# Normalising u on three engines instead of one: statistics on VectorE and GpSimd, scaling on ScalarE, modulation on VectorE, in pairs of blocks

## The chip, the cores and the metric

The kernel runs on one core of a Trainium2 chip. Its time is the device time of one execution in microseconds; each comparison takes the median of some runs of each kernel on the same chip. Traces come from one profiled execution.

## What is computed

A token mixer (a state-space convolution, "S4") and a channel mixer, each behind a layer norm that is modulated by a condition vector. Cut to what matters here:

```python
x = A_u                                              # 1 x 2048 x 512
mod = (silu(c) @ w_mod).reshape(1, 6, 1, -1)
sa, ca, ga, sb, cb, gb = (mod[:, k] for k in range(6))
h = layernorm(x) * (1 + ca) + sa                     # the part that the change touches
x = x + ga * ssm(h, ...)                             # K = Re sum C exp(dt A l) dB; y = irfft(rfft(K) rfft(h)) + h Dskip
h = layernorm(x) * (1 + cb) + sb
x = x + gb * mixer(h, w1, w2, w3, w4)                # shifts, two matmuls, two more with gelu
```

## The kernel before

The convolution is done in the frequency domain, with the transforms as matmuls. **The first stage** (to about 213 us of the span) makes the kernel K of the convolution and the first transform of u; the stages behind it (spectra, inverse transform, mixer, channel matmuls) begin with the last matmuls of the first and are not touched.

The order of the instructions is written out by hand (`tc.manual_schedule()`): each engine runs its own list from front to back, and an instruction that waits holds up all behind it. The first stage is a loop over 33 steps `k`. In step k stand, in this order:

- what an earlier step has put into `later` (on ScalarE, "ACT": the eviction `KX<-kp` of the last bursts, the evictions `vs<-pu` of a transform of u with their stores to VU, the modulation's rows `wm` and `modg`);
- `turns(k + 2)`: 18 matmuls on TensorE ("PE", lines 457 and 458) into two PSUM tiles `xx` (two buffers), and two sines on ACT, `tr<-xx`, that read them;
- in steps 1, 5, 9, ... 25 the exponentials for the next four steps: five times two matmuls (lines 251 and 256) and five activations `p<-xx`, a table load before and one behind them, with some matmuls of `fill` (line 491) that keep PE busy;
- `products(k)` on VectorE ("DVE"): two operations at line 475, in even steps one at 481, and one each at 484 and 485; they write `e0` and `e1` (two buffers each);
- `burst(k)` on PE: 64 small matmuls (line 507) that read them;
- after step 3, 7, ... 27 a small product of weights on DVE (line 263, `weigh`);
- `side[k]`: work hung on this step by a table.

u is held as 16 blocks of 128 x 512, four to a tile `ut[g]` ("xu"), two tiles at a time. Per block `side` has `u_stats` (DVE: `bn_stats`, `bn_aggr`, lines 146 and 147; GpSimd, "POOL": add eps and a power, lines 149 and 150), two steps later `u_norm` (DVE, lines 424 and 425: subtract the mean and multiply by 1 + ca, multiply by 1/sigma and add sa), and per pair of blocks two transforms `u_dft` (PE, line 434), one in each of the next two steps. When the second pair and the fourth pair have been transformed, `load_u` reloads the tile (four transfers of 256 KB on SyncE's queue, line 237). The steps:

```python
at = lambda i: 1 + (i * 28) // 16
for i in range(16):
    side[max(at(i) - 2, 0)].append(lambda i=i: u_stats(i))
    side[at(i)].append(lambda i=i: u_norm(i))
    if i % 2 == 1:
        side[at(i) + 1].append(lambda i=i: u_dft(i - 1, 0))
        side[at(i) + 2].append(lambda i=i: u_dft(i - 1, 1))
    if i % 4 == 3 and i < 8:
        side[at(i) + 2].append(lambda i=i: load_u(i // 4 + 2))
```

Behind step 31's products PE runs eight warming matmuls (line 497), the last burst and four more.

Of the kernel before, what the change touches and what calls it, by code (L numbers as in the profile page):

```python
# [7 lines left out]
F32 = mybir.dt.float32  # L8
F32R = mybir.dt.float32r
I32 = mybir.dt.int32  # L10
AF = mybir.ActivationFunctionType
OP = mybir.AluOpType
# [94 lines left out]
def dram(t, off, ap):  # L107
    return bass.AP(tensor=t.tensor, offset=t.offset + off, ap=ap)


def body(ctx, tc, A):
    nc = tc.nc
    V, S, P, T, Y = nc.vector, nc.scalar, nc.gpsimd, nc.tensor, nc.sync
    pool = lambda name, bufs=1, **k: tc.tile_pool(name=name, bufs=bufs, **k)
    glob = ctx.enter_context(pool("glob"))
    dpool = ctx.enter_context(pool("dscr", space=DRAM))

    def act(out, in_, f=AF.Copy, scale=1.0, bias=0.0):
        return S.activation(out, in_, f, bias=bias, scale=scale)  # L119
# [11 lines left out]
    eps_t = glob.tile([128, 8], F32, name="eps_t")  # L131
    V.memset(eps_t, 1e-5)
    pw = glob.tile([128, 8], F32, name="pw")
    V.memset(pw, -0.5)
    m_one = glob.tile([128, 8], F32, name="m_one")
    V.memset(m_one, -1.0)
    mv1 = glob.tile([128, 16, 2], F32, name="mv1")
    rs1 = glob.tile([128, 16], F32, name="rs1")
    st1 = glob.tile([128, 10, 2, 6], F32, name="st1")

    def ln_stats(pl, xs, tag):
        n = len(xs)
        st = pl.tile([128, n, 6], F32, name=tag + "s")
        mv = pl.tile([128, n, 2], F32, name=tag + "m")
        for i, x in enumerate(xs):
            V.bn_stats(st[:, i], x)
            V.bn_aggr(mv[:, i], st[:, i])
        r = pl.tile([128, n], F32, name=tag + "r")
        P.tensor_tensor(r, mv[:, :, 1], eps_t[:, :n], op=OP.add)
        P.tensor_tensor(r, r, pw[:, :n], op=OP.pow)  # L150
        return mv, r

    def exp_exact(pl, x, shape, name, scale=1.0):
        t = lambda s, dt=F32: pl.tile(shape, dt, name=f"{name}_{s}")
# [47 lines left out]
    mods = [modu[:, k] for k in range(3)] + [modg[:, k] for k in range(3)]  # L202
# [29 lines left out]
    ut = {}  # L232

    def load_u(g):
        x = ut[g] = up.tile([128, 4, 512], F32, name="xu")
        for bp in range(4):
            Y.dma_start(x[bp * 32:(bp + 1) * 32],
                        dram(A["u"], (bp * 16 + g * 4) * 512, [[64 * 512, 32], [1, 2048]]))
# [45 lines left out]
    with tc.manual_schedule():  # L284
# [89 lines left out]
        at, at0 = tmp("at"), tmp("at0")  # L374
# [36 lines left out]
    wk = a1.enter_context(pool("wk", bufs=2, reuse_waits="tile"))  # L411
# [4 lines left out]
    ul = {}  # L416

    def u_stats(b):
        ul[b] = ln_stats(wk, [ut[b // 4][:, b % 4]], "lu")

    def u_norm(b):
        x = ut[b // 4][:, b % 4]
        mv, r = ul.pop(b)
        V.scalar_tensor_tensor(x, x, mv[:, 0, 0:1], mods[1], op0=OP.subtract, op1=OP.mult)
        V.scalar_tensor_tensor(x, x, r[:, 0:1], mods[0], op0=OP.mult, op1=OP.add)

    def u_dft(b, cp2):
        x = ut[b // 4]
        ps = [psu.tile([128, 512], F32, name="pu") for h in range(2)]
        for i in range(2):  # L430
            for h in range(2):
                q = 64 * (1 - i if h == 0 else i)
                j = slice(32 * JB[2 * h + cp2], 32 * JB[2 * h + cp2] + 32)
                T.matmul(ps[h][q:q + 64], FU[j, h, cp2 * 64:cp2 * 64 + 64], x[j, b % 4 + i],
                         start=True, stop=True, skip_group_check=True)

        def evict():
            vs = uv.tile([128, 2, 512], F32, name="vs")
            for h in range(2):
                act(vs[:, h], ps[h])  # L440
                c0 = h * 32 + cp2 * 16 + (14 - b if h == 0 else b)
                for i in range(2):
                    Y.dma_start(dram(VU, (c0 + i) * 256, [[16384, 64], [1048576, 2], [1, 256]]),
                                vs[i * 64:i * 64 + 64, h].rearrange("p (a d) -> p a d", a=2))
        later.append(evict)
# [69 lines left out]
    side = {k: [] for k in range(40)}  # L515
    for k in range(8):
        w, i = ("w3", k) if k < 4 else ("w4", k - 4)
        n = A[w].shape[0] // 4
        side[4 + 3 * k].append(lambda w=w, i=i * n, n=n: P.dma_start(WD[w][i:i + n], A[w][i:i + n]))
    for n in range(3, 6):  # L520
        k = 7 * n - 9
# [1 line left out]
        side[k].append(lambda n=n: later.append(mod_parts(n)))  # L523
        side[k + 1].append(lambda n=n: later.append(mod_sum(n)))
    at = lambda i: 1 + (i * 28) // 16
    for i in range(16):
        side[max(at(i) - 2, 0)].append(lambda i=i: u_stats(i))
        side[at(i)].append(lambda i=i: u_norm(i))
        if i % 2 == 1:
            side[at(i) + 1].append(lambda i=i: u_dft(i - 1, 0))  # L530
            side[at(i) + 2].append(lambda i=i: u_dft(i - 1, 1))
        if i % 4 == 3 and i < 8:
            side[at(i) + 2].append(lambda i=i: load_u(i // 4 + 2))

    def add_skip(h, g0, g1):
        V.tensor_add(Kq[:, h, g0:g1, 31], DS[:, h * 64 + g0:h * 64 + g1], Kq[:, h, g0:g1, 31])
# [114 lines left out]
    def spectrum_k(jh, kc):  # L651
        p = [psa.tile([128, 2, 2, 128], F32, name="pk2") for gh in range(2)]
        for i in range(2):
            for ro in range(2):
                for ri in range(2):
                    for kk in range(2):
                        for gh in range(2):
                            k1 = kc * 4 + 2 * kk + i
                            rows = slice(gh * 64, gh * 64 + 64)
                            w = T2[k1 // 16][rows, k1 % 16]  # L660
                            if ri == gh:
                                w = w[:, ro * 64:ro * 64 + 64]
                            elif ro == ri:
                                w = w[:, gh * 64:gh * 64 + 64]
                            else:
                                w = T3[rows, k1]
                            T.matmul(p[gh][kk * 64:kk * 64 + 64, i, ro], w,
                                     VK[jh][rows, ri * 32 + k1].rearrange("p j g -> p (j g)"),
                                     start=(ri == 0), stop=(ri == 1), skip_group_check=True)
        return p  # L670
# [115 lines left out]
    def transposed(x):  # L786
        ps = [psT.tile([128, 2, 256], F32, name=f"pT{j}") for j in range(2)]
        for k in range(4):
            for i in range(2):
                T.transpose(ps[k // 2][:, k % 2, i * 128:i * 128 + 128], x[:, i, k * 128:k * 128 + 128], ident)  # L790
        return ps

    def parts_of(ps):
        hi = [cm.tile([128, 2, 256], F32R, name=f"nh{j}") for j in range(2)]
        lo = [cm.tile([128, 2, 256], F32R, name=f"nl{j}") for j in range(2)]
        for j in range(2):
            act(hi[j], ps[j])
            V.tensor_sub(lo[j], ps[j], hi[j].bitcast(F32))  # L798
        return [hi[k // 2][:, k % 2] for k in range(4)], [lo[k // 2][:, k % 2] for k in range(4)]
# [283 lines left out]
    with tc.manual_schedule():  # L1083
# [12 lines left out]
        for n, st in enumerate(steps):  # L1096
            p = spectrum_k(*st)
# [126 lines left out]
        n = cm.tile([128, 2, 512], F32, name="h2")  # L1224
        sm = [(cm.tile([128, 2], F32, name="cmv"), cm.tile([128, 1], F32, name="crs")) for i in range(2)]
# [17 lines left out]
        r = transposed(n)  # L1243
        split_w(1)
        r = parts_of(r)
# [4 lines left out]
        for g in range(8):  # L1250
            r = chan(g, r)
# [18 lines left out]
```

## Time and profile before

| | |
|---|---|
| median of 3 runs | 717.22 us (712.0 to 718.76) |
| the profiled execution | 716.82 us, span 715.1 us |
| PE matmul, PE weight load | 671.7 us (94%), 520.1 us (73%) |
| DVE | 506.3 us (71%) |
| ACT | 335.6 us (47%) |
| POOL | 85.6 us (12%) |
| granted PE clock | 0.993 on average |

The shares are means over the span. In the first stage DVE, ACT and PE are all far busier than the means of DVE and ACT say, so a table of stretches of 20 us is read before the page's totals. In timelines each row has its start in us, its length in us, engine, line, operation, output and input, the count, and in brackets the idle time before it with what ended it. Line 119 is the helper of all activations; these are told apart by their tiles.

### The profile page before, as it was taken

The numbers are of one execution on the slowest core, as the hardware profiler recorded it, in microseconds if no ns is written. First come the engines' busy times: TensorE is split into PE (matmuls) and PEld (weight loads), VectorE is DVE, ScalarE is ACT, GpSimd is POOL, SyncE is SP. The second block draws the span as 40 slices with busy tenths as digits, with TensorE's granted clock in tenths as the row PEclk, the third lists the DMA queues.
The fourth block names the chain that finished last, engine by engine and source line by source line (L and its number), as shares of the span: only waits on it lengthen the run. The fifth ranks groups of instructions, "written<-read, shape, count | busy, mean of one in ns | idle before, by whom it ended". The sixth has DMA issues, their size and how long they took to land.

```text
span 715.1 us, 16869 instructions
## 1 busy us (share of the span) xinstructions
PE 671.7 (94%) x7083; PEld 520.1 (73%) x7083; DVE 506.3 (71%) x847; ACT 335.6 (47%) x549; POOL 85.6 (12%) x191
## 2 busy tenths in 40 slices
PE   2689999999999899998899999999999999999997
PEld 1356655666568566664688889989898998989896
DVE  8989999999986566767978868557463635454422
ACT  2768898889956255634245623313123121212121
POOL 1011212112000001100463200201010000000000
PEclk9999999999999999999999999999999999999999
DMA  8452274744439999793649402011020111111011
GB/s 286 152 129 69 74 217 102 191 128 116 132 80 266 232 289 315 224 324 144 217 149 302 132 5 56 15 45 31 16 74 16 49 27 31 31 30 30 0 30 31
DMA packets 56884, 85.52 MB, mean 120 GB/s; under 512 B 5764, under 2 KB 43656, under 8 KB 55144
## 3 DMA queue, kind: packets, MB, share of 16 engines
q1 hardware_dynamic: 52648, 66.61, 34.8%
q0 software_dynamic: 3136, 16.52, 6.4%
q10 hardware_dynamic: 1024, 1.31, 0.6%
q8 instruction: 56, 0.92, 0.5%
q14 instruction: 20, 0.16, 0.1%
HBM read 58.20 MB, written 31.85 MB: 126 GB/s over the span
## 4 chain that ended last, share of the span: by engine, by line
PE 48%; DVE 2%; ACT 1%; DMA 1%; SPq 0%; issue 0%; POOL 0%; DVEq 0%; ACTq 0%
PE pm L825 7%; PE pm L828 7%; PE pm L826 7%; PE pa L949 6%; PE pa L941 6%; PE pa L942 5%; PE ph L879 2%; PE ph L880 2%; PE ph L882 2%; PE pT L790 2%; DMA ld<-ZT 1%; PE pT L1140 1%; PE py L722 1%; ACT nh L119 0%; DVE st L758 0%; SPq L707 0%
## 5 line engine op out<-in xcount | busy, mean ns | idle before, releaser
L119 ACT ACTIVATE gh<-pm 128x512 fp32r<-128x512 f32 (+1 forms) x48 | 26.9, 560 | 200.7 <-PE pm L828 200.7
L825 PE MATMUL pm<-nh,w3h 128*128 128x256 f32 (+1 forms) x352 | 85.8, 279 | 0.9 <-ACT nh L119 0.9
L826 PE MATMUL pm<-nh,w3l 128*128 128x256 f32 (+1 forms) x352 | 85.6, 279 | 0.1
L933 DVE TENSOR_TENSOR gl<-gf,gh 128x512 fp32r<-128x512 f32 (+1 forms) x48 | 30.8, 642 | 68.4 <-ACT gf L119 68.4
L941 PE MATMUL pa<-w4h,gh 128*128 128x512 f32 (+1 forms) x176 | 69.6, 396 | 0.0
L942 PE MATMUL pa<-w4l,gh 128*128 128x512 f32 (+1 forms) x176 | 68.9, 392 | 0.0
L825 PEld LDWEIGHTS pm<-nh,w3h 128*128 128x128 f32 (+1 forms) x352 | 65.3, 185 | 2.6 <-ACT nh L119 1.1
L826 PEld LDWEIGHTS pm<-nh,w3l 128*128 128x128 f32 (+1 forms) x352 | 65.2, 185 | 2.2 <-DVE w3l L744 0.5
L828 PE MATMUL pm<-nl,w3h 128*128 128x256 f32 (+1 forms) x352 | 54.8, 277 | 0.0
L949 PE MATMUL pa<-w4h,gl 128*128 128x512 f32 (+1 forms) x176 | 48.1, 391 | 0.8 <-DVE gl L933 0.8
L458 PE MATMUL xx<-MG,ON 64*128 64x512 f32 x160 | 48.0, 396 | 0.0
L457 PE MATMUL xx<-MG,ON 64*128 64x512 f32 x160 | 48.0, 396 | 0.0
L828 PEld LDWEIGHTS pm<-nl,w3h 128*128 128x128 f32 (+1 forms) x352 | 46.7, 185 | 0.2 <-DVE nl L798 0.2
L753 POOL TENSOR_TENSOR rs<-mv,eps_t 128x1 f32<-128x1 f32 (+1 forms) x39 | 11.4, 293 | 279.0 <-DVE mv L759 266.6
L678 DVE TENSOR_TENSOR ma<-pk,us 128x512 f32<-128x512 f32 x32 | 21.9, 685 | 30.7 <-issue 22.9
L119 ACT ACTIVATE z<-pz 128x512 f32<-128x512 f32 x32 | 17.5, 595 | 54.6 <-PE pz L693 38.3
L885 DVE TENSOR_TENSOR h<-h,ph 128x512 f32<-128x512 f32 x16 | 11.0, 686 | 45.2 <-PE ph L882 45.2
L475 DVE SCALAR_TENSOR_TENSOR e<-tr,p 128x512 f32<-128x512 f32 x64 | 41.0, 682 | 2.1 <-ACT tr L119 1.9
L949 PEld LDWEIGHTS pa<-w4h,gl 128*128 128x128 f32 (+1 forms) x176 | 33.0, 188 | 8.3 <-DVE gl L933 1.2
L484 DVE TENSOR_TENSOR e<-tr,p 128x1024 f32<-128x1024 f32 x32 | 38.9, 1217 | 0.0
L507 PEld LDWEIGHTS kp<-e,e 128*32 128x32 f32 x2048 | 30.0, 110 | 12.2 <-issue 8.1
L485 DVE TENSOR_TENSOR e<-tr,m 128x1024 f32<-128x1024 f32 x32 | 38.9, 1216 | 0.0
(234 smaller groups left out, 1763.5 us busy)
## 6 DMA issues: line engine op xcount, KB each, us to landing
VU<-vs SPq DMA_DIRECT2D x64, 128.0 KB, 3.5
ld<-VU SPq DMA_DIRECT2D x32, 256.0 KB, 10.4
ZT<-z POOLq DMA_DIRECT2D x15, 512.0 KB, 8.3
ld<-ZT SPq DMA_DIRECT2D x12, 512.0 KB, 8.2
Dw<-in_w POOLq DMA_DIRECT2D x8, 688.0 KB, 4.7
xu<-in_u SPq DMA_DIRECT2D x16, 256.0 KB, 6.8
KX<-in_u SPq DMA_DIRECT2D x16, 256.0 KB, 10.2
GD<-go SPq DMA_DIRECT2D x16, 256.0 KB, 2.3
```

The lines of the kernel that those rows point to most:

```text
L119: return S.activation(out, in_, f, bias=bias, scale=scale)
L457: T.matmul(x[:, :512], la, ma, start=(i == 0), stop=(i == len(ops) - 1))
L458: T.matmul(x[:, 512:], lb, mb, start=(i == 0), stop=(i == len(ops) - 1))
L475: V.scalar_tensor_tensor(e0[:, 1, a], tr[:, 1, 0], 1.0 - 2.0 * a, mg[:, a], op0=OP.mult, op1=OP.mult)
L484: V.tensor_mul(e0[:, 0], tr[:, 0, 0:1].to_broadcast([128, 2, 512]), mg)
L485: V.tensor_mul(e1.rearrange("p r d q -> p r (d q)"), tr[:, :, 1], m1s[0][:, u % 2:u % 2 + 1].to_broadcast([128, 2, 512]))
L825: T.matmul(p, wh[:, k, c], hi[k], start=(k == 0), stop=False)
L826: T.matmul(p, wl[:, k, c], hi[k], start=False, stop=False)
L828: T.matmul(p, wh[:, k, c], lo[k], start=False, stop=(k == 3))
L941: T.matmul(acc[i], gh[:m, e, s], W4h[:m, f], start=(f == 0), stop=False)
L942: T.matmul(acc[i], gh[:m, e, s], W4l[:m, f], start=False, stop=False)
L949: T.matmul(acc[i], gl[:m, e, s], W4h[:m, f], start=False, stop=(f == 10))
```

## The change

The normalising is done per pair p of blocks (2p, 2p + 1), eight pairs. DVE only runs `bn_stats`; POOL makes mean and variance from its two halves, 1/sigma, and minus mean over sigma, in ten small operations; ACT applies both to each block (`u_scale`, Identity with a scale and a bias per partition, in place); DVE multiplies the pair by 1 + ca and adds sa in two operations of 128 x 1024 (`u_mod`). The pair's steps: statistics in step q and the one behind it (the first pair's both in step 0), scaling in step o - 1, modulation in step o, transforms in o + 1 and o + 2, reload in o + 2 for the pairs 1 and 3. q is 0, 1, 3, 7, 11, 14, 17, 21 and o is 5, 7, 9, 13, 16, 20, 23, 27. So the first pair's transforms go from steps 3 and 4 to 6 and 7, the second's from 7 and 8 to 8 and 9, and its reload from 8 to 9; all other transforms stay.

```diff
+    lnc = glob.tile([128, 5], F32, name="lnc")
+    for i, v in enumerate((0.5, 1.0 / 512, 1e-5, -0.5, -1.0)):
+        V.memset(lnc[:, i:i + 1], v)
...
     def u_stats(b):
-        ul[b] = ln_stats(wk, [ut[b // 4][:, b % 4]], "lu")
-
-    def u_norm(b):
-        x = ut[b // 4][:, b % 4]
-        mv, r = ul.pop(b)
-        V.scalar_tensor_tensor(x, x, mv[:, 0, 0:1], mods[1], op0=OP.subtract, op1=OP.mult)
-        V.scalar_tensor_tensor(x, x, r[:, 0:1], mods[0], op0=OP.mult, op1=OP.add)
+        p, i = divmod(b, 2)
+        if i == 0:
+            ul[p] = [wk.tile([128, 2, n], F32, name=f"lu{n}", bufs=3) for n in (6, 2, 1, 3)]
+        st, sm, d, rn = ul[p]
+        V.bn_stats(st[:, i], ut[b // 4][:, b % 4])
+        if i == 1:
+            t = lambda o, x, y, op: P.tensor_tensor(o, x, y, op=op)
...
+            t(rn[:, :, 0:1], rn[:, :, 0:1], c(3), OP.pow)
+            t(rn[:, :, 2:3], sm[:, :, 0:1], c(4), OP.mult)
+            t(rn[:, :, 1:2], rn[:, :, 2:3], rn[:, :, 0:1], OP.mult)
+
+    def u_scale(p):
+        rn = ul.pop(p)[3]
+        for i in range(2):
+            x = ut[p // 2][:, p % 2 * 2 + i]
+            act(x, x, AF.Identity, scale=rn[:, i, 0:1], bias=rn[:, i, 1:2])
+
+    def u_mod(p, k, op):
+        x = ut[p // 2][:, p % 2 * 2:p % 2 * 2 + 2]
+        V.tensor_tensor(x, x, mods[k][:, None].to_broadcast([128, 2, 512]), op=op)
...
-    for i in range(16):
...
+    for p in range(8):
+        o = at(2 * p + 1) + (3, 1, 0, 0, 0, 0, 0, 0)[p]
+        q = (0, 1, 3, 7, 11, 14, 17, 21)[p]
+        side[q].append(lambda p=p: u_stats(2 * p))
+        side[q + (p > 0)].append(lambda p=p: u_stats(2 * p + 1))
+        side[o - 1].append(lambda p=p: u_scale(p))
+        side[o].append(lambda p=p: u_mod(p, 1, OP.mult))
+        side[o].append(lambda p=p: u_mod(p, 0, OP.add))
+        side[o + 1].append(lambda p=p: u_dft(2 * p, 0))
+        side[o + 2].append(lambda p=p: u_dft(2 * p, 1))
+        if p in (1, 3):
+            side[o + 2].append(lambda p=p: load_u(p // 2 + 2))
```

How ACT's list stands around step 22, behind the exponentials of step 21 (`TABLE_LOAD`, `turn`): before,

```order
L119 ACT_TABLE_LOAD
L119 ACTIVATE turn_370<-hpi 128x1
L119 ACTIVATE KX<-kp 128x8x64
L119 ACTIVATE vs<-pu 128x512 x2
L119 ACTIVATE tr<-xx 128x1024
L119 ACTIVATE tr<-xx,hpi 128x1024
L119 ACTIVATE vs<-pu 128x512 x2
```

and with the change:

```order
L119 ACT_TABLE_LOAD
L119 ACTIVATE turn_376<-hpi 128x1
L119 ACTIVATE KX<-kp 128x8x64
L119 ACTIVATE vs<-pu 128x512 x2
L119 ACTIVATE tr<-xx 128x1024
L119 ACTIVATE tr<-xx,hpi 128x1024
L119 ACTIVATE xu<-xu,lu_1998 128x512 x2
L119 ACTIVATE vs<-pu 128x512 x2
```

The two `tr` are the sines of step 24. The scaling of pair 6 (`xu<-xu,lu`) has come in behind them; pairs 1 and 7 stand in the same way behind the sines of steps 8 and 28.

DVE's list between the products of steps 23 and 24, before,

```order
L485 TENSOR_TENSOR e_2428<-tr,m_2350 128x1024
L263 TENSOR_TENSOR p_2232<-p_2232,WN 128x64x4
L424 SCALAR_TENSOR_TENSOR xu<-xu,lum,modu 128x512
L425 SCALAR_TENSOR_TENSOR xu<-xu,lur,modu 128x512
L146 BN_STATS lus<-xu 128x6
L147 BN_AGGR lum<-lus 128x2
L475 SCALAR_TENSOR_TENSOR e_2499<-tr,p_2236 128x512 x2
```

and with the change (line 497 is 485 of before, 254 is 263, 487 is 475, 437 is `u_mod`):

```order
L497 TENSOR_TENSOR e_2464<-tr,m_2375 128x1024
L254 TENSOR_TENSOR p_2259<-p_2259,WN 128x64x4
L437 TENSOR_TENSOR xu<-xu,modu 128x1024 x2
L487 SCALAR_TENSOR_TENSOR e_2528<-tr,p_2263 128x512 x2
L493 TENSOR_TENSOR m_2532<-p_2259 128x1024
```

One block's normalising and another's statistics have made room for the modulation of a pair, which stands ahead of step 24's products.

SyncE's queue from the second pair's stores to the reload of the first tile, before,

```order
L443 DMA VU<-vs 64x2x256 x12
L213 DMA wm<-in_wm 128x4x512
L237 DMA xu<-in_u 32x2048 x4
L443 DMA VU<-vs 64x2x256 x16
L213 DMA wm<-in_wm 128x4x512
```

and with the change:

```order
L455 DMA VU<-vs 64x2x256 x8
L204 DMA wm<-in_wm 128x4x512
L455 DMA VU<-vs 64x2x256 x4
L228 DMA xu<-in_u 32x2048 x4
L455 DMA VU<-vs 64x2x256 x16
L204 DMA wm<-in_wm 128x4x512
```

The reload of u (`xu<-in_u`) has gone four stores further back, to behind the transform of step 9, and no longer follows the 1 MB load of `wm` directly.

More of the change, by code (lines that the diff above doesn't have):

```diff
@@ L139, in body @@
     st1 = glob.tile([128, 10, 2, 6], F32, name="st1")
[L141 to L151, printed above, removed]
     def exp_exact(pl, x, shape, name, scale=1.0):
@@ L418, in u_stats @@
     def u_stats(b):
-        ul[b] = ln_stats(wk, [ut[b // 4][:, b % 4]], "lu")
-    def u_norm(b):
-        x = ut[b // 4][:, b % 4]
-        mv, r = ul.pop(b)
-        V.scalar_tensor_tensor(x, x, mv[:, 0, 0:1], mods[1], op0=OP.subtract, op1=OP.mult)
-        V.scalar_tensor_tensor(x, x, r[:, 0:1], mods[0], op0=OP.mult, op1=OP.add)
+        p, i = divmod(b, 2)
[5 more added lines that the diff above has]
+            t = lambda o, x, y, op: P.tensor_tensor(o, x, y, op=op)
+            c = lambda q: lnc[:, None, q:q + 1].to_broadcast([128, 2, 1])
+            t(sm, st[:, :, 1:3], st[:, :, 4:6], OP.add)
+            t(sm, sm, lnc[:, None, 0:2].to_broadcast([128, 2, 2]), OP.mult)
+            t(d, st[:, :, 1:2], st[:, :, 4:5], OP.subtract)
+            t(d, d, c(0), OP.mult)
+            t(d, d, d, OP.mult)
+            t(rn[:, :, 0:1], sm[:, :, 1:2], d, OP.add)
+            t(rn[:, :, 0:1], rn[:, :, 0:1], c(2), OP.add)
+            t(rn[:, :, 0:1], rn[:, :, 0:1], c(3), OP.pow)
[9 more added lines that the diff above has]
+        V.tensor_tensor(x, x, mods[k][:, None].to_broadcast([128, 2, 512]), op=op)
     def u_dft(b, cp2):
@@ L525, in body @@
     at = lambda i: 1 + (i * 28) // 16
-    for i in range(16):
[L527 to L533, printed above, removed]
+    for p in range(8):
[10 more added lines that the diff above has]
+            side[o + 2].append(lambda p=p: load_u(p // 2 + 2))
     def add_skip(h, g0, g1):
```

## The prediction

> **What bounds the kernel now.** I read the table of stretches first. The change sits in the first stage, which ends at about 213 us with the last burst of matmuls. Columns: PE, PEld, DVE, ACT and POOL busy, PEclk, DMA.
>
> ```profile
> 80.00:100.00 20.00, 19.34 (x352) 12.95 (x353) 19.67 (x29) 16.75 (x21) 5.39 (x8) 0.91 0.46 133
> 120.00:140.00 20.00, 19.96 (x358) 12.72 (x346) 19.70 (x26) 17.96 (x23) 3.63 (x6) 1.00 0.50 140
> ```
>
> DVE is busy 19.7 of 20 us, PE 19 to 20, ACT 17 to 18: three engines are nearly full at once. Which of them sets the end is read from the timeline at the end of the stage.
>
> ```profile
> 209.78 1.21 DVE L485 TENSOR_TENSOR e<-tr,m 128x1024 f32<-128x1024 f32 x1
> 207.93 1.10 PE L507 MATMUL kp<-e,e 128*32 128x64 f32 x64
> 208.96 2.11 PE L497 MATMUL xx<-CE,TES 128*128 128x512 f32 x8
> 211.04 1.10 PE L507 MATMUL kp<-e,e 128*32 128x64 f32 x64
> ```
>
> DVE's last product ends at 209.78 + 1.21 = 210.99, and the last burst starts at 211.04. But PE comes to it from eight warming matmuls that end at 211.07: both arrive together. So DVE and PE bound the stage jointly, and a shorter DVE alone leaves PE's list where it is.
>
> Below, P(k) is step k's products on DVE, burst(k) the matmuls that read them, tr(k) the two sines of step k, which ACT makes in step k - 2. In steps 1, 5, 9, ... 25 ACT also does five exponentials between two table loads, so that tr(8), tr(24) and tr(28), made right after such a block, come latest.
>
> **The change part by part.**
>
> ```profile
> L424 DVE SCALAR_TENSOR_TENSOR xu<-xu,lum,modu 128x512 f32<-128x512 f32 x16 | 11.9, 743 | 0.0
> L425 DVE SCALAR_TENSOR_TENSOR xu<-xu,lur,modu 128x512 f32<-128x512 f32 x16 | 12.0, 752 | 1.8
> L147 DVE BATCH_NORM_AGGREGATE lum<-lus 128x2 f32<-128x6 f32 x16 | 2.9, 182 | 0.6
> L146 DVE BATCH_NORM_STATS2 lus<-xu 128x6 f32<-128x512 f32 x16 | 11.0, 685 | 0.0
> L484 DVE TENSOR_TENSOR e<-tr,p 128x1024 f32<-128x1024 f32 x32 | 38.9, 1217 | 0.0
> L119 ACT ACTIVATE h<-h,nm,rs 128x512 f32<-128x512 f32 x16 | 12.8, 813 | 26.8 <-POOL nm L815 26.8
> L150 POOL TENSOR_TENSOR lur<-lur,pw 128x1 f32<-128x1 f32 x16 | 13.9, 872 | 1.3
> L149 POOL TENSOR_TENSOR lur<-lum,eps_t 128x1 f32<-128x1 f32 x16 | 8.5, 531 | 149.3 <-DVE lum L147 149.3
> 358.54 1.51 ACT L119 ACTIVATE h<-h,nm,rs 128x512 f32<-128x512 f32 x2
> ```
>
> DVE loses 16 x (743 + 752 + 182) ns = 26.8 us and gets 16 products of 128x1024; L484 has the same shape and also a broadcast operand, 1217 ns: 19.5 us. Saved: 7.3 us. The statistics stay at 685 ns a block. ACT gets 16 activations with scale and bias from SBUF; the later stage has the very form (h<-h), two in 1.51 us, so 8 x 1.51 = 12.1 us on an engine with some 2 us free in 20. It needs no new table load: ACT's list has 18 before and after. Pool gets ten small operations a pair, nine at about 0.53 and a power at 0.87: some 5.6 us, hidden behind the three or more steps (of about 5.2 us) between statistics and scaling; without that cover the scaling would wait those 5.6 us. The early statistics therefore remove a wait for Pool. The five constants are memsets of the prologue, costed at nothing beside its loads.
>
> What is added on the path is another wait: DVE's modulation of pair p now waits for ACT's scaling, and ACT's list has the scaling of pairs 1, 6 and 7 right behind tr(8), tr(24) and tr(28), the late ones. Behind the waiting modulation stands P(8), P(24) or P(28), whose sines are by then long there. So such a P starts after tr's end + 1.51 (scaling) + 2.5 (two dependent products: 1.22 + 1.22 and the gap of 0.1 that stands below between L424's end and L425) = 4.0 us. Step 24 as it is:
>
> ```profile
> 171.46 0.42 DVE L263 TENSOR_TENSOR p<-p,WN 128x256 f32<-128x256 f32 x1
> 171.79 0.74 DVE L424 SCALAR_TENSOR_TENSOR xu<-xu,lum,modu 128x512 f32<-128x512 f32 x1
> 172.65 0.75 DVE L425 SCALAR_TENSOR_TENSOR xu<-xu,lur,modu 128x512 f32<-128x512 f32 x1
> 172.95 1.14 ACT L119 ACTIVATE tr<-xx,hpi 128x1024 f32<-128x1024 f32 x1
> 173.95 1.12 ACT L119 ACTIVATE vs<-pu 128x512 f32<-128x512 f32 x2
> 174.14 1.28 DVE L475 SCALAR_TENSOR_TENSOR e<-tr,p 128x512 f32<-128x512 f32 x2
> 177.61 1.22 DVE L485 TENSOR_TENSOR e<-tr,m 128x1024 f32<-128x1024 f32 x1
> 179.06 1.10 PE L507 MATMUL kp<-e,e 128*32 128x64 f32 x64
> ```
>
> DVE fills the time from 171.46 + 0.4 with normalising and starts P(24) at 174.14, as tr(24) ends (172.95 + 1.14 = 174.09). P(24) ends at 178.83, burst(24) follows at 179.06: 0.2 us to spare. After: 174.09 + 4.0 + 4.7 (P's length, 174.14 to 178.83) = 182.8, so burst(24) is some 3.7 us later. Steps 8 and 28:
>
> ```profile
> 70.11 1.09 PE L434 MATMUL pu<-xu,FU 32*64 32x512 f32 x8
> 82.72 1.01 ACT L119 ACTIVATE tr<-xx 128x1024 f32<-128x1024 f32 x1
> 91.66 1.10 PE L507 MATMUL kp<-e,e 128*32 128x64 f32 x64
> 194.57 1.14 ACT L119 ACTIVATE tr<-xx,hpi 128x1024 f32<-128x1024 f32 x1
> 194.73 1.29 DVE L475 SCALAR_TENSOR_TENSOR e<-tr,p 128x512 f32<-128x512 f32 x2
> ```
>
> Step 8: the two transforms of the first pair (the second at 70.11, 1.0 us each to the next start) move from steps 3 and 4 to 6 and 7, so PE, and ACT behind it, reaches step 5's exponentials 2.0 us earlier. The second tr(8) then ends at 82.72 + 0.9 + 1.0 - 2.0 = 82.6; scaling and modulation bring 86.6, one block's statistics (0.7) 87.3, P(8) 92.0, against burst(8) at 91.66: the head start is gone, **+0.4 us**.
>
> Step 12: the load of the third group of u waits for the second pair's last transform, which moves from step 8 to step 9, where it stands behind the exponentials' matmuls; and the statistics that need this load move up from step 13 to 11.
>
> ```profile
> 97.91 1.10 PE L507 MATMUL kp<-e,e 128*32 128x64 f32 x64
> 101.91 0.51 PE L251 MATMUL xx<-CE,TES 128*128 128x512 f32 x2
> 113.66 1.10 PE L507 MATMUL kp<-e,e 128*32 128x64 f32 x64
> 95.00 2.04 SPq L237 DMA_DIRECT2D xu<-in_u  x4
> DMA to landing us min/median/max: 4.9/6.8/7.7
> ```
>
> Burst(9) at 97.91 + 0.4 = 98.3, exponentials to 102.42 + 0.4 = 102.8, transform to 103.9, the last of four issues 1.5 us on at 105.4. Landing takes 4.9 to 7.7 us; I take 5.8, below the median, since the 1 MB load of weights that goes right before this one now goes four stores earlier: 111.2. DVE stands until then. Statistics 0.7, P(12) 4.7: 116.6 against burst(12) at 113.66, **+2.9 in all, 2.5 of it new**. The fourth group's load (issued in step 15, wanted in step 17) is as tight as this; I take nothing for it, and at most the third's 2.5.
>
> Step 24: 174.09 + 2.9 + 4.0 + 4.7 = 185.7 against 179.06, **+6.6, 3.7 new**. Step 28: tr(28) ends at 195.71, + 6.6 + 4.0 = 206.3 against P(28)'s start at 194.73, **+11.6, 5.0 new**. From there DVE has only products, 194.73 to 210.99 before, and the last burst waits for them: the stage ends 11.6 us late. The 7.3 us that DVE saves lie in its waits. The later stages start from that burst and shift whole.
>
> **Bounds.** The scaling pair costs 1.12 (the vs pair above) to 1.63 us (two of 0.813): -1.2 to +0.4 over three places. The landing at 4.9 or 7.7 us: -0.9 or +1.9, and the fourth load 0 to +2.5. Then PE's clock:
>
> ```profile
> 80.00:82.00 2.00, 1.82 (x10) 1.51 (x12) 1.97 (x6) 1.98 (x3) 1.00 (x2) 0.63 0.00 0
> 82.00:84.00 2.00, 2.00 (x10) 1.13 (x8) 2.00 (x3) 1.73 (x4) 0.98 (x2) 0.52 0.67 220
> 244.49 0.61 PE L667 MATMUL pk<-VK,xu 64*64 64x128 f32 x4 [3.12 <-issue]
> 244.00:246.00 2.00, 1.51 (x29) 0.59 0.96 228
> 246.00:248.00 2.00, 2.00 (x42) 0.56 1.01 336
> ```
>
> The granted clock is about 0.55 for 3.5 us after a gap of 3.12 us in stage two, and once in this stage without such a gap; half a clock for 3.5 us costs PE about 1.6 us. The change gives PE waits of 2 to 4 us at bursts 8, 12, 24 and 28, each of them a candidate. I take one such stretch beyond those of before, **+1.5**, with none to four as ends (0 to +6.2).
>
> [...]
>
> **Sum.** 0.4 + 2.5 + 3.7 + 5.0 + 1.5 = 13.1 us. The profiled execution took 716.82 us (span 715.1), the median of the runs is 717.22: 716.82 + 13.1 = **729.9**.
>
> **Rivals.**
> *No further half clock* (0.20): 11.6 alone, 728.4. For it: waits here are mostly under 3.12 us.
> *A half clock after every wait* (0.14): 11.6 + 4 x 1.5 = 17.6, 734.4. For it: those two stretches; against: at step 28 DVE sets the end and hides it.
> *The waits are absorbed* (0.20): ACT has 2 to 3 us free in 20; if scaling lands in that free time, or PE is far enough behind DVE at these bursts, only the 2.9 of step 12 is left: 719.7. Against: at bursts 24 and 31 the slack is 0.2 and 0.0.
> *The saving arrives* (0.08, the other side): DVE would end 7.3 us earlier, at 709.5 if PE followed. PE can't follow that far: its rows stand end to end but for two waits for ACT at each of seven exponential blocks,
>
> ```profile
> 97.25 0.73 PE L256 MATMUL xx<-CE,TES 32*128 32x512 f32 x2 [0.46 <-ACT tr L119]
> 102.76 0.50 PE L457 MATMUL xx<-C,T0S 64*128 64x512 f32 x1 [0.34 <-ACT p L119]
> ```
>
> so 7 x 0.8 = 5.6 us in all. Half of that gives 714.0. It decides if tr(24) and tr(28) come over 4 us earlier against DVE than now.
> *The change doesn't do what it says*: the statistics are indeed early, but the modulation waits for the scaling, which is not; this is the forecast's mechanism.
>
> **Chances.** The forecast with one stretch has 0.38. A measurement of this kernel can tell about 1%, 7.2 us, from no change (the three runs spread from 712.0 to 718.76). Slower by over 1% (above 724.4) are the forecast and the first two rivals, 0.72; faster by over 1% (below 710) only the extreme of the last, 0.03; within 1% 0.25. The likeliest case's own range is 725 to 736; with the absorbed case in it the range is 717 to 736.
>
> **What would show it.** Right: DVE, gap-free before, idle 2 to 7 us before the modulations of pairs 1, 6 and 7, released by ACT xu, and 3 to 5 us before the statistics of step 11, released by the load; PE waiting on DVE's products at bursts 8, 12, 24 and 28; the stage ending near 225 us; ACT with 16 activations xu<-xu of 0.8 us; Pool about 22 us busier, waited for by nobody. Wrong: DVE still at 19.7 of 20, or a last burst before 215 us.

## The result and the profile after

The changed kernel takes **741.71 us** (median of 4 runs, 735.49 to 743.66) against 717.22 before: ratio **1.034** (95% interval 1.030 to 1.038). Run again in a later comparison it took 738.49 us against 717.37, ratio 1.026 (1.019 to 1.033). One of those four runs, 743.03 us, counts as slow and is left out of the ratio and of the means below. The profiled execution took 735.49 us, span 733.7, granted clock 0.984 (before: 716.82, 715.1, 0.993). Slower was foretold; the median lies 11.8 us above the forecast and 5.7 above the range.

In the changed file the products stand at lines 487 to 497 (before 475 to 485), the bursts at 519 (507), the warming matmuls at 509 (497), statistics, Pool's chain and modulation at 414, 416 and 437. The table of stretches, after; columns PE, PEld, DVE, ACT, POOL busy, PEclk, DMA:

```profile
80.00:100.00 20.00, 17.25 (x284) 11.07 (x280) 17.72 (x21) 14.94 (x21) 6.34 (x3) 0.83 0.46 130
120.00:140.00 20.00, 17.63 (x287) 10.75 (x291) 19.97 (x24) 18.48 (x24) 14.11 (x14) 1.00 0.24 68
200.00:220.00 20.00, 17.37 (x293) 10.34 (x286) 13.80 (x16) 16.14 (x21) 0.00 (x0) 0.97 0.12 30
```

Before, the last slice that lies wholly in the stage was:

```profile
180.00:200.00 20.00, 19.52 (x305) 11.41 (x296) 19.60 (x26) 18.13 (x23) 1.45 (x2) 1.00 0.32 78
```

Where three engines were nearly full, PE now has 17 to 18 of 20 us. DVE has 17.7 in the first of these slices and 13.8 in the last, with the waits of steps 8 and 28; between 120 and 140 us it is as full as before. The groups of the first stage, after: busy, mean ns of one, then idle before and its releaser.

```profile
L437 DVE TENSOR_TENSOR xu<-xu,modu 128x1024 f32<-128x1024 f32 x16 | 19.6, 1223 | 11.1 <-ACT xu L119 10.8
L119 ACT ACTIVATE xu<-xu,lu 128x512 f32<-128x512 f32 x16 | 12.3, 828 | 0.0
L414 DVE BATCH_NORM_STATS2 lu<-xu 128x6 f32<-128x512 f32 x16 | 10.9, 684 | 13.1 <-DMA xu<-in_u 13.1
L416 POOL TENSOR_TENSOR lu<-lu 128x2 f32<-128x2 f32 (+1 forms) x32 | 41.5, 1297 | 92.8 <-DVE lu L414 91.5
```

The prices of the operations came as taken: 19.6 us for the products on DVE (taken 19.5), 12.3 for ACT's scaling (12.1). What is new is the idle time: DVE waits 10.8 us for ACT's scaling, at three places, and 13.1 us for two loads of u. The table of waits (total, times, longest) carries this over to PE:

```profile
PE kp L519 <- DVE e L497: 13.2, 6, 3.2
```

The end of the stage, from the timeline:

```profile
229.04 1.22 DVE L497 TENSOR_TENSOR e<-tr,m 128x1024 f32<-128x1024 f32 x1
228.53 2.10 PE L509 MATMUL xx<-CE,TES 128*128 128x512 f32 x8
230.56 1.10 PE L519 MATMUL kp<-e,e 128*32 128x64 f32 x64
```

The last burst starts at 230.56, 19.5 us later than before; 18.6 us of that is in the span. So the loss of the profiled execution lies in the first stage. The starts of single bursts (rows kp<-e,e of 64 matmuls in the timelines) show where it arises. The last three columns are counted from burst(0), which itself lies between 48.66 and 51.98 us in the profiles of this document:

| burst | before, us | after, us | after later by | new since the row above | foretold |
|---|---|---|---|---|---|
| 0 | 48.66 | 49.69 | 0 | | |
| 8 | 91.66 | 92.94 | 0.25 | 0.25 | 0.4 |
| 9 | 97.91 | 102.18 | 3.24 | 3.0 | 1.5, place open |
| 12 | 113.66 | 121.89 | 7.20 | 4.0 | 2.5 |
| 20 | 157.39 | 167.52 | 9.10 | 1.9 | 0 (bound 2.5) |
| 24 | 179.06 | 192.81 | 12.72 | 3.6 | 3.7 |
| 31 | 211.04 | 230.56 | 18.49 | 5.8 | 5.0 |

### The profile page after: what moved, and what is told of

Its sections match the earlier page's. It is cut to its first block, busy times and chain, and to the rows that moved or that the text cites. A ratio compares the mean times of both kernels' runs of the same rounds, so it can differ in the third digit from the quotient of the medians.

```text
span 733.7 us, 16893 instructions
## 1 busy us (share of the span) xinstructions
PE 681.5 (93%) x7083; PEld 526.1 (72%) x7083; DVE 500.7 (68%) x820; ACT 344.3 (47%) x565; POOL 139.1 (19%) x239
## 3 DMA queue, kind: packets, MB, share of 16 engines
q10 hardware_dynamic: 1024, 1.31, 0.6%
## 4 chain that ended last, share of the span: by engine, by line
PE 45%; DVE 3%; DMA 2%; POOL 1%; ACT 1%; SPq 1%; issue 1%; ACTq 0%; DVEq 0%; POOLq 0%
PE pm L844 7%; PE pm L842 7%; PE pm L841 7%; PE pa L965 5%; PE pa L958 5%; PE pa L957 5%; PE ph L895 2%; PE ph L898 2%; PE ph L896 2%; PE pT L806 1%; DMA GD<-go 1%; PE py L738 1%; DMA ld<-ZT 0%; SPq L754 0%; POOL rs L770 0%
## 5 line engine op out<-in xcount | busy, mean ns | idle before, releaser
L841 PE MATMUL pm<-nh,w3h 128*128 128x256 f32 (+1 forms) x352 | 87.3, 281 | 0.9 <-ACT nh L119 0.9
L842 PE MATMUL pm<-nh,w3l 128*128 128x256 f32 (+1 forms) x352 | 87.3, 281 | 0.1
L416 POOL TENSOR_TENSOR lu<-lu 128x2 f32<-128x2 f32 (+1 forms) x32 | 41.5, 1297 | 92.8 <-DVE lu L414 91.5
L844 PE MATMUL pm<-nl,w3h 128*128 128x256 f32 (+1 forms) x352 | 56.4, 282 | 0.0
L470 PE MATMUL xx<-MG,ON 64*128 64x512 f32 x160 | 49.8, 409 | 0.0
L469 PE MATMUL xx<-MG,ON 64*128 64x512 f32 x160 | 49.8, 408 | 0.0
L519 PE MATMUL kp<-e,e 128*32 128x64 f32 x2048 | 36.4, 224 | 13.2 <-DVE e L497 13.2
L694 DVE TENSOR_TENSOR ma<-pk,us 128x512 f32<-128x512 f32 x32 | 21.9, 686 | 25.6 <-issue 18.6
```

The source lines that it names most:

```text
L416: t = lambda o, x, y, op: P.tensor_tensor(o, x, y, op=op)
L469: T.matmul(x[:, :512], la, ma, start=(i == 0), stop=(i == len(ops) - 1))
L470: T.matmul(x[:, 512:], lb, mb, start=(i == 0), stop=(i == len(ops) - 1))
L519: T.matmul(kp[32 * j:32 * j + 32, (k % 2) * 4 + g], e1[:, r, d], e0[:, r, :, d * 32:d * 32 + 32], start=(r == 0), stop=(r == 1), skip_grou ...
L841: T.matmul(p, wh[:, k, c], hi[k], start=(k == 0), stop=False)
L842: T.matmul(p, wl[:, k, c], hi[k], start=False, stop=False)
```

## The experiments

All of them change one thing in the kernel before or after. The length of the stage is the time from burst(0) to burst(31) of the profiled execution: 162.4 us before, 180.9 after, and 181.1 in the changed kernel's second profile.

> The changed kernel once more, with a profile. Both theories: 735 to 744 us. In the first profile the last burst started at 230.6 us (before: 211.0). If that execution was a lucky one, this profile shows the missing 5 us as further stretches at half the granted clock, or as a later landing of the loads of u.

738.49 us against 717.37 before: slower again, by 2.6%, though the interval now reaches below 2%. The stage of this profile is as long as the first one's and its waits are the same (PE's for DVE 13.3 us, DVE's for loads 13.2, for the scaling 10.8). Its span is 3.2 us longer, of which 1.3 lie ahead of burst(0) (50.96 us against 49.69) and 1.8 behind the last burst. Two other runs with this start (pairs 6 and 7 alone, the other table of steps) have burst(0) at 51.00 us and two half-clock stretches ahead of it, 36 to 40 and 46 to 50 us, where the first profile has one (45 to 48).

**The wait for the scaling taken away.** The scaling of pairs 1, 6 and 7 writes elsewhere, so that the modulation waits for nothing; the work on each engine is the same, and the result lacks the scaling of these pairs.

```diff
+    usx = wk1.tile([128, 512], F32, name="usx")
...
-            act(x, x, AF.Identity, scale=rn[:, i, 0:1], bias=rn[:, i, 1:2])
+            if p in (1, 6, 7):
+                act(usx, WN, AF.Identity, scale=rn[:, i, 0:1], bias=rn[:, i, 1:2])
+            else:
+                act(x, x, AF.Identity, scale=rn[:, i, 0:1], bias=rn[:, i, 1:2])
```

> The scaling of pairs 1, 6 and 7 stays at its place in ACT's list but reads and writes other tiles, so the modulation of these three pairs waits for nothing (the result lacks their scaling). Theory (queue wait): DVE's waits before steps 8, 24 and 28 vanish, and with them 1 to 4 us at step 8, 3.7 at step 24 and 5.8 at step 28: 10 to 15 us below the changed kernel, 727 to 732, last burst at 216 to 221 us. Rival (ACT has no room for 16 more activations): ACT's list is as long as before, DVE waits for the sines instead, and the time stays within 3 us of the changed kernel.

720.38 us, ratio 1.006 (1.002 to 1.009); stage 164.7 us. Of the loss of 18.5 us in the stage, 16.2 go with three waits. DVE's waits in this kernel:

```profile
DVE lu L414 <- DMA xu<-in_u: 7.9, 2, 4.0
DVE xu L442 <- ACT xu L119: 0.2, 1, 0.2
```

That is more than the theory gave back: the granted clock is 1.00 in every slice of 20 us from 60 to 240 us, and DVE's waits for loads have fallen from 13.1 to 7.9 us. ACT does all of its added work here, so its capacity is not the bound.

**The load's wait taken away.** The statistics of blocks 8 and 12 read an older block, which is there.

```diff
-        V.bn_stats(st[:, i], ut[b // 4][:, b % 4])
+        V.bn_stats(st[:, i], ut[b // 4 - (b in (8, 12))][:, b % 4])
```

> The statistics of blocks 8 and 12 read a block that is long there, so that DVE doesn't wait in steps 11 and 17 for the reloads of u (the result has wrong statistics for two blocks). Theory (late load): DVE's 8.4 and 4.7 us of waiting go, PE's bursts 12 and 18 come 4.0 and 1.3 us earlier: 4 to 6 us below the changed kernel. Rival (the wait lies in slack that the later waits for ACT swallow again): under 2 us.

738.01 us, ratio 1.027 (1.021 to 1.033), stage 182.0: nothing gained. The timeline of this kernel around step 12 shows why.

```profile
103.82 1.71 SPq L228 DMA_DIRECT2D xu<-in_u  x4
106.21 12.84 SPq L455 DMA_DIRECT2D VU<-vs  x12
114.75 1.09 ACT L119 ACTIVATE vs<-pu 128x512 f32<-128x512 f32 x2 [2.75 <-DMA VU<-vs]
119.19 2.48 DVE L437 TENSOR_TENSOR xu<-xu,modu 128x1024 f32<-128x1024 f32 x2 [2.80 <-ACT xu L119]
120.61 0.73 PE L247 MATMUL xx<-CE,TES 32*128 32x512 f32 x2 [1.37 <-ACT tr L119]
```

The stores of VU stand behind the reload in SP's queue. ACT's eviction into one of two `vs` buffers waits for them until 114.75, so the scaling behind it is late, and DVE, which no longer waits for the load, waits 2.80 us for that scaling. PE's clock is then halved for 10.2 us, to 132 us. The load wait was the first of two in a row.

**Both taken away.**

> Both of these together. Theory: all of the loss goes, 15 to 20 us below the changed kernel, 720 to 726 us, and no gain on before, since PE paces the stage. Rival (the saving of 7.3 us on DVE then arrives): below 712 us. Rival (ACT's length is the loss): above 735 us.

720.95 us, ratio 1.0045 (1.002 to 1.007), stage 163.0. Without these waits the kernel is level with the one before, and not faster: DVE's saved 7 us don't arrive, which fits a PE list as long as it was. Against the run with the scaling's waits alone taken away (720.38 us) the loads' waits are worth nothing that the runs can tell.

**Only pair 1, only pairs 6 and 7** (the first edit above, for `p == 1` and for `p in (6, 7)`).

> The changed kernel, with the scaling of pair 1 alone writing to a tile that nobody reads (pair 1 goes unscaled); same work on ScalarE and VectorE. Theory by the stage's own account (the wait at step 8 brings 0.3 us, a half-clock stretch at 92 to 99 us of 3 us and some of the load wait): burst 12 at 115 to 117 us instead of 121.9, and 4 to 7 us less than the changed kernel's 739, 732 to 735. Rival (the later waits grow by what the first gives back): 737 to 741.

> The changed kernel, with the scaling of pairs 6 and 7 alone writing to a tile that nobody reads (they go unscaled); same work on ScalarE and VectorE. Theory by the stage's own account (3.6 us at step 24, 5.8 us at step 28 and in the stretch behind it): bursts up to 20 as in the changed kernel, burst 31 at 220 to 223 us instead of 230.6, and 7 to 10 us less than 739, 729 to 732. Rival (half-clock stretches come elsewhere instead): 734 to 739.

Pair 1: 732.36 us, ratio 1.024 (1.020 to 1.028), stage 175.3, burst(12) at 115.08. Pairs 6 and 7: 729.09, ratio 1.020 (1.014 to 1.025), stage 172.6, burst(31) at 223.60. The stage gets 5.6 and 8.3 us shorter; together 13.9, against 16.2 with all three. So the places nearly add up. With pair 1 alone freed, burst(12) starts 65.12 us after burst(0), against 65.00 before and 72.20 in the changed kernel: the whole loss up to step 12 goes with that one wait. The stage gets back less, since burst(24) is then followed by half clock (186 to 190 us).

**Warming matmuls before the four bursts.**

```diff
+                if k in (8, 12, 24, 28):
+                    warm(8)
                 burst(k, *e)
```

> The changed kernel with eight warming matmuls more on TensorE ahead of bursts 8, 12, 24 and 28, where it waits 2.6 to 3.3 us for VectorE's products; they write the scratch tile that the other warming matmuls write and nobody reads them. Theory (part of the loss is TensorE's clock, which drops after those waits): the half-clock stretches at 92 to 99 us and 218 to 226 us go, burst 9 starts within 2 us of its new due time (98 to 101 instead of 102.2), the lost clock of the run falls from 12.6 us to about 6 and the time from about 739 to 731 to 736. Rival (the waits alone are the loss and the stretches come anyway): the eight matmuls (1.7 us each time) change nothing or lengthen the path, 739 to 742.

740.41 us, ratio 1.033 (1.028 to 1.038), stage 183.4: no gain. A slice behind step 8, one from a new half-clock stretch, and the burst ahead of that stretch:

```profile
94.00:96.00 2.00, 2.00 (x42) 1.01 (x32) 2.00 (x3) 0.52 (x2) 2.00 (x1) 1.00 0.93 335
162.00:164.00 2.00, 2.00 (x10) 1.16 (x8) 2.00 (x4) 1.09 (x2) 2.00 (x1) 0.50 0.00 0
```

```profile
159.61 1.10 PE L519 MATMUL kp<-e,e 128*32 128x64 f32 x64 [2.42 <-DVE e L497]
```

The half clock behind step 8 is gone: burst(9) starts 49.54 us after burst(0), against 52.49 in the changed kernel, so a stretch there was worth 3.0 us. But others came, behind a wait of 2.27 us at 118.21 and one of 2.42 us at 159.61. The first of these is a wait of the warming matmuls themselves: they write an `xx` tile and wait for ACT's sines to be done with it. In all, the half clock between burst(0) and the last burst is 10.2 us long here, against 13.6 in the changed kernel, and yet the stage is 2.5 us longer. So this run moved the stretches and lengthened the path, and it doesn't isolate what the half clock costs.

**ScalarE's load alone, and the moved transforms alone**, both in the kernel before.

```diff
+    usx = wk1.tile([128, 512], F32, name="usx")
+    def u_extra():
+        for i in range(2):
+            act(usx, WN, AF.Identity, scale=eps_t[:, 0:1], bias=pw[:, 0:1])
+    for o in (5, 7, 9, 13, 16, 20, 23, 27):
+        side[o - 1].append(u_extra)
```

> The kernel before, with sixteen activations of 128x512 added to ScalarE at the places where the changed kernel scales u (two a pair); they read a constant tile, write a tile that nobody reads, and nobody waits for them. Rival (ScalarE's capacity is the bound: 12 us more work on an engine that is nearly full): 727 to 730, bursts after 8, 24 and 28 later by 1.5 us each. Theory (only the order DVE waits - ACT scales - DVE modulates costs): the activations fall into ScalarE's free time or delay only its sines, which have slack at most places: 717 to 721.

719.65 us against 718.14, ratio 1.001 (0.998 to 1.004), stage 162.3. The sixteen activations took as long as the scaling does:

```profile
L119 ACT ACTIVATE usx<-WN,pw,eps_t 128x512 f32<-128x512 f32 x16 | 13.1, 817 | 0.3
```

13 us of work on ACT cost nothing that the runs can tell, at the same places and with nobody waiting for it.

```diff
+        o = at(i) + {1: 3, 3: 1}.get(i, 0)
-            side[at(i) + 1].append(lambda i=i: u_dft(i - 1, 0))
+            side[o + 1].append(lambda i=i: u_dft(i - 1, 0))
 ...
```

> The kernel before with only the placing of the first two pairs changed as in the change: their normalising and transforms three and one steps later, and with the second pair the reload of u; the normalising itself, and which engine does it, stays. The statistics of the later blocks are where they were. Theory (the later reload is worth nothing by itself and the moved transforms cost nothing): 716 to 719, burst 12 at 113 to 115 us. Rival (the late reload or the transforms' new place costs by itself): 720 to 724, burst 12 at 116 or later, DVE waiting for the load of the third group.

720.63 us, ratio 1.005 (1.002 to 1.008), stage 164.0, burst(12) at 116.74. The edit moves only the transforms and the reload; the normalising of these pairs, which the recorded text names too, stays where it was. The time lies at the near end of the rival's range and burst(12) in it, but DVE waits for no load here. The profile has two half-clock stretches, at 74 to 86 us, where the kernel before has one. How much of the 0.5% comes from the moved transforms and how much from that stretch stays open; it is small beside the change's 3%.

**Another table of steps**, with each scaling one to three steps ahead of its modulation.

```diff
+    steps_u = ((0, 0, 4, 5, 6), (1, 2, 4, 6, 7), (3, 4, 8, 9, 10), (7, 8, 12, 13, 14),
+               (13, 14, 16, 17, 18), (14, 15, 19, 20, 21), (19, 20, 22, 24, 25), (21, 22, 24, 27, 28))
+    for p, (q0, q1, s, m, f) in enumerate(steps_u):
...
```

> The changed kernel's normalising (ScalarE scales, Pool does the small operations) with a table of steps in which each scaling stands one to three steps ahead of its modulation and no modulation stands in a step whose sines come right after a block of exponentials. Theory (the place of the modulation behind a late scaling is the whole loss): DVE waits for ScalarE's scaling under 1 us in all, no half-clock stretch between 88 and 230 us, 716 to 722. Rival one (the saving of DVE's 7 us arrives once nothing waits): 708 to 712. Rival two (the longer ScalarE and Pool work costs by itself, wherever it stands): 730 or more.

734.01 us, ratio 1.023 (1.019 to 1.027), stage 178.4: a miss, and a time in the second rival's range. The waits that the table was to take away are still there: DVE waits 9.7 us for ACT's scaling, at four places (3.58 us at 100.83, 3.15 at 147.43). Nor had I looked at anything but the modulation. Two pairs scaled one after the other in step 4 hold up the sines that PE waits for at 75 us (1.62 us), and around step 16 the timeline has a chain that I had not thought of:

```profile
136.29 8.05 POOL L416 TENSOR_TENSOR lu<-lu,lu 128x2 f32<-128x2 f32 x1
145.88 1.52 ACT L119 ACTIVATE xu<-xu,lu 128x512 f32<-128x512 f32 x2 [2.10 <-POOL lu L416]
148.36 2.22 PE L247 MATMUL xx<-CE,TES 32*128 32x512 f32 x4 [2.44 <-ACT tr L119]
```

One of Pool's small operations takes 8.05 us, ACT waits for Pool with the sines queued behind, PE waits 2.44 us for them, and its clock is halved for 13.7 us. Pool's work, hidden in the change, isn't hidden with a step less of room.

**Three scalings one step earlier.** All is computed; the scaling of pairs 1, 6 and 7 comes right behind the exponentials, ahead of the late sines.

```diff
-        side[o - 1].append(lambda p=p: u_scale(p))
+        side[o - 1 - (p in (1, 6, 7))].append(lambda p=p: u_scale(p))
```

> The changed kernel with one thing moved: ScalarE scales pairs 1, 6 and 7 one step earlier, right behind the block of exponentials and ahead of the late sines of steps 8, 24 and 28, instead of behind them; all is computed. VectorE can then modulate while ScalarE makes the sines. Theory (the whole loss is the place of those three scalings in ScalarE's list): the sines come 1.5 us later than before and nothing else, the waits for xu at 85, 186 and 211 us fall under 0.5 us, no half-clock stretch between 88 and 200 us, 719 to 725. Rival (the load of u and Pool's stretched small operations cost by themselves): 729 to 735.

**721.81 us** against 715.37, ratio 1.009 (1.006 to 1.012); stage 166.4. Step 8 in its timeline:

```profile
81.29 1.50 ACT L119 ACTIVATE xu<-xu,lu 128x512 f32<-128x512 f32 x2
83.18 1.01 ACT L119 ACTIVATE tr<-xx 128x1024 f32<-128x1024 f32 x1
84.08 1.11 ACT L119 ACTIVATE tr<-xx,hpi 128x1024 f32<-128x1024 f32 x1
82.91 2.48 DVE L437 TENSOR_TENSOR xu<-xu,modu 128x1024 f32<-128x1024 f32 x2
85.90 1.27 DVE L487 SCALAR_TENSOR_TENSOR e<-tr,p 128x512 f32<-128x512 f32 x2
```

DVE modulates without a gap while ACT makes the sines, and its products follow at 85.90. One expression changed in the order takes back 14.5 of the stage's 18.5 us, with the same operations on every engine, Pool's included: the rival that the load and Pool's work cost by themselves (729 to 735) fell. The 6 us that stay against the kernel before were not taken apart. The expectation missed one point: at step 28 DVE still waits 2.50 us (197.43 us), since there the exponentials themselves end late (194.47 us, with a table load of 1.28 us behind them).

**And the statistics one step later** for blocks 8, 9, 12 and 13 (q of pairs 4 and 6: 12 and 18 instead of 11 and 17).

> The kernel of the run before (three scalings one step earlier), and the statistics of blocks 8, 9 and 12, 13 one step later, so that VectorE comes to them after their load has landed. Theory (the load is hidden once the scalings are early): within 2 us of the run before, VectorE's waits for the load under 4 us in all instead of 8 to 13. Rival (the load wait costs, and now goes): 3 to 5 us less, 716 to 719. Second rival (Pool's small operations come too late for the scaling of pair 4): ScalarE waits for Pool at step 15, 3 to 6 us more.

727.48 us, ratio 1.017 (1.014 to 1.020), stage 172.3. DVE's wait for loads falls from 7.9 to 1.8 us and the time rises by 5.7. That is the size of the second rival, but ACT waits for Pool nowhere: none of the three theories has it. As where the load's wait was taken away, ACT waits for the stores of VU (4.22 us at 115.42), DVE for the scaling (4.28 us at 119.86), and the clock is halved from 122 to 133 us. No version here beats the kernel before.

## Why the forecast was right in sign and too small

**Step 24 and step 28: right.** Step 28 after, from the timeline:

```profile
208.33 1.14 ACT L119 ACTIVATE tr<-xx,hpi 128x1024 f32<-128x1024 f32 x1
209.32 1.54 ACT L119 ACTIVATE xu<-xu,lu 128x512 f32<-128x512 f32 x2
210.90 2.49 DVE L437 TENSOR_TENSOR xu<-xu,modu 128x1024 f32<-128x1024 f32 x2 [5.87 <-ACT xu L119]
213.30 1.29 DVE L487 SCALAR_TENSOR_TENSOR e<-tr,p 128x512 f32<-128x512 f32 x2
218.05 1.20 PE L519 MATMUL kp<-e,e 128*32 128x64 f32 x64 [2.63 <-DVE e L497]
```

The sines end at 209.47 and the products start at 213.30: 3.8 us, where 4.0 was taken. Step 24 brought 3.6 us (3.7 foretold) and steps 28 to 31 5.8 (5.0). The mechanism, a modulation that waits behind late sines with the next products queued behind it, is shown: three moved scalings take most of it away and bring back most of the time.

**Step 8: right** (0.25 us, 0.4 foretold), the head start of 2.0 us included: in the run without the three waits, burst(8) starts 40.94 us after burst(0), against 43.00 before.

**The half clock: the step that failed.** "I take one such stretch beyond those of before, +1.5." The first wait, at step 8, was already followed by one:

```profile
92.94 1.94 PE L519 MATMUL kp<-e,e 128*32 128x64 f32 x64 [2.75 <-DVE e L497]
```

```profile
92.00:94.00 2.00, 1.06 (x40) 1.06 (x44) 2.00 (x4) 0.83 (x2) 0.42 (x1) 0.66 0.83 201
94.00:96.00 2.00, 2.00 (x44) 0.94 (x32) 2.00 (x4) 0.00 (x0) 2.00 (x1) 0.50 1.00 369
96.00:98.00 2.00, 2.00 (x10) 1.09 (x8) 2.00 (x2) 1.09 (x2) 2.00 (x1) 0.50 0.15 55
98.00:100.00 2.00, 2.00 (x14) 1.44 (x12) 1.97 (x4) 1.03 (x1) 1.92 (x3) 0.64 0.53 127
```

The burst took 1.94 us instead of 1.10. The four slices lack 0.34, 0.50, 0.50 and 0.36 of their clock, 3.4 us in all, so the clock was halved for 6.8 us, not 3.5: 3.0 us lost. I had read the length of a stretch from two short ones of the kernel before. Over the profiles here that were read in slices of 2 us, the stretches that end before their execution does are 3.4 us long (80 to 84 us in the kernel before), 6.8 (this one), 10.2 (122 to 134 us with the statistics moved) or 13.7 (148 to 164 us with the other table of steps), worked out in the same way: a short one and its multiples. A second long one (219 to 226 us) cost only 0.6, since DVE set the end there, as the rival text said. These 0.6 are a wait of DVE for a burst that was late:

```profile
226.70 1.29 DVE L487 SCALAR_TENSOR_TENSOR e<-tr,p 128x512 f32<-128x512 f32 x2 [0.62 <-PE kp L519]
```

So in the profiled execution this term measured 3.6 us in the stage. And that execution is a mild one, inside the range. If (1 - clock) x span is the clock time lost, it lost 11.7 us; the two slowest runs of its comparison (743.47 and 743.66 us, clock 0.973 and 0.975) lost 20.0 and 18.5. The seven runs of the changed kernel that count have a mean of 738.8 us and 13.6 us lost, 45 runs of the kernel before 717.1 and 6.3. A line through the former gives 0.88 us of time for each such us, one through the latter 0.57. So **some 4 to 6 of the 22 us between the means are half clock, where 1.5 was taken**; this alone would have brought the forecast to 733 to 735. It is a worked-out share, not one taken away by itself, and it is for the whole span: in which stage the slower runs lost their clock is not known. In the profiled execution the 18.5 us of the stage are 5.4 more than the 13.1 of the sum: 2.1 of them are half clock (3.6 where 1.5 was taken), 3.4 lie at the loads, and the rest cancels to 0.1.

Which waits were followed by half clock doesn't go by their length. Waits of 2.75 (burst 8) and 2.63 us (burst 28) were followed by it, waits of 3.25 (burst 12) and 2.81 us (burst 24) in the same execution were not; the second profile has its stretches at the same two places (bursts of 1.94 us at 94.21 and of 1.40 us at 226.60). With pair 1 freed, burst(24) waits 2.80 us and a stretch does come (184 to 190 us); with pairs 6 and 7 freed, burst(8) waits 2.78 us and one comes (94 to 102), burst(12) waits 3.33 us and none does; and with the load's wait taken away the 10.2 us up to 132 us have no single wait of over 1.4 us just ahead of them. So the length of the wait doesn't decide it; what does stays open.

The recorded range was also narrower than its own bounds: 11.6 with 6.2 for four stretches, 1.9 for the landing, 2.5 for the fourth load and 0.4 for the scaling reaches 739.4, not 736.

**The loads: too small, and not to be added up.** The third group's load made 4.0 us instead of 2.5, and the fourth 1.9 instead of nothing:

```profile
107.80 3.90 SPq L228 DMA_DIRECT2D xu<-in_u  x4
116.54 0.69 DVE L414 BATCH_NORM_STATS2 lu<-xu 128x6 f32<-128x512 f32 x1 [8.40 <-DMA xu<-in_u]
153.16 0.69 DVE L414 BATCH_NORM_STATS2 lu<-xu 128x6 f32<-128x512 f32 x1 [4.67 <-DMA xu<-in_u]
```

The four issues took 3.90 us, not 1.5, and started at 107.80 instead of 103.9. The later start is the half clock ahead of them and the 1.0 us by which this execution's burst(0) was later. DVE's wait was 8.4 us, where 3 to 5 had been foretold. With pair 1 freed, and so without that half clock, burst(9) to burst(12) took 17.9 us, against 15.8 before and 19.7 in the changed kernel: 2.1 us for the third load, near the 2.5 taken. The 1.9 us up to burst(20) can't be put down to the fourth load with certainty, since burst(12) to burst(20) took 44.9 us with the loads' and the scaling's waits both taken away and 45.0 with the scaling's alone, against 43.7 before. Taking the loads' waits away brought nothing that the times can tell, with the late scalings or without them (1.7 us of the stage in the latter case). I had added up waits of one chain as if each could be had by itself.

**The rivals.** The absorbed waits and the saving that arrives fell with the result; that ACT's free time would take the scaling is true for the work (sixteen activations cost nothing) and false for the wait. "A half clock after every wait" was nearest (734.4): two of the four waits were hit, and in the profiled execution they cost 3.0 and 0.6 us instead of 1.5 each.

## What to carry to other kernels

When work moves to another engine, price its place in that engine's list and not its duration: 13 us of activations were free, and three pairs of them behind late sines cost 16 us of the stage. Look for what stands just ahead of the moved instruction and what is queued behind the one that waits for it; moving the three by one step gave most of it back. In this stage TensorE's new waits for VectorE's products came to 13.2 us, where the stage lost 18.5, and at two of four places 6.8 us of half clock followed, which cost 3.0 and 0.6 us. So take the length and the number of such stretches from a spread of runs, and keep ranges open on that side.

## What was not expected of the hardware

The same small operation of Pool takes very different times. In the changed kernel's timeline:

```profile
159.15 9.51 POOL L416 TENSOR_TENSOR lu<-lu 128x4 f32<-128x4 f32 x1 [10.09 <-DVE lu L414]
167.38 2.48 DVE L437 TENSOR_TENSOR xu<-xu,modu 128x1024 f32<-128x1024 f32 x2
```

An addition of four columns, 0.56 us at other places (138.00), lasts 9.51 us here, while some ten DVE instructions follow one another without a gap. At 138.00 DVE was at work too, so DVE's work alone doesn't settle it; what makes the operation long was not tried and stays open. In all, Pool is 53.5 us busier than before (139.1 against 85.6), where 22 was foretold. In the change nobody waits for it; in the other table of steps, ACT waited 2.10 us.
